# Requesting expert weights into places of the first stage as they come free, and storing the last logits from ScalarE's queue

## The chip, the cores and the metric

The kernel runs on one core of one Trainium2 chip. The metric is the device time of one execution in microseconds (us); the median of several executions is given. TensorE is called PE, VectorE DVE, ScalarE ACT, GpSimd POOL and SyncE SP, as in the profile.

## The reference, cut to what matters

Three parts follow one another, all in float32 (`w_gate`, `w_val` and `w_out` arrive as float64).

```
X = rfft(x, axis=1); y = irfft(X * (filt_r + 1j*filt_i), n=3072)   # x: 8 x 3072 x 256
logits = y @ phi                                                   # 24576 tokens, 32 slots
slot_in = softmax(logits, over tokens).T @ y                       # 32 x 256, 8 experts x 4 slots
slot_out[e] = relu(slot_in[e] @ w1[e]) @ w2[e]                     # w1: 256 x 1024, w2: 1024 x 256 each
z = softmax(logits, over slots) @ slot_out                         # 24576 x 256
out = (silu(z @ w_gate) * (z @ w_val)) @ w_out                     # 256 -> 1536 -> 256
```

The slots need the logits of all tokens, so the experts cannot start until the whole first part is done, and the last part cannot start until the experts are done.

## The kernel before, in words

The program is written in the order in which each engine is to run it (`tc.manual_schedule`): every engine, and each DMA queue with the engine that issues it, takes its own instructions strictly in the order of the text. A DMA that SP issues has SP wait until what the DMA needs is there, and all that SP has still to issue stands behind it.

**First stage, `phase1` (L131).** Sixteen steps (a batch of eight and half of the 256 columns each) of six units, so 96 units, numbered `i` in the loop at L690. A unit does one sixth of a step's spectrum (`s2_unit`, `tr_unit`, `phi_pair`); beside it, units 1 to 4 of a step transform the next step's x (`s1_chunk`, `spread`). x stands in two places `xp[0]` and `xp[1]` (16 KB of each partition), its transforms in `bp[0]` and `bp[1]` (12 KB), with two staging tiles `sgp` (4 KB) between. Three kinds of work are threaded into the units as generators:

- `chain(b)` (L307): for each batch the logits, their maximum, exponentials and slot sums. `pump` (L665) moves it one step on. Its step at L400 to L405 stores the batch's logits to DRAM (`lgd`) in four DMAs on SP's queue.
- `conv` (L558): turns w_gate, w_val and w_out into float32 in DRAM, 12 chunks each, 36 in all. A chunk is four calls: two DVE operations (L584, L585), three ACT operations (L587 to L589), one DVE operation (L591), then two POOL operations, the store on SP's queue and the load of the chunk after next (L593 to L596). One more call at the beginning loads the first two chunks.
- `first_weights` (L599): the softmax over slots of the first batch, 16 calls, after `conv`.

`aside` (L686) makes one call of the generator that is first in the list `side`; a call that finds its generator at the end does no work and takes it off the list. Before the change a unit from 8 on makes one call at L698 and a second at L712 while `conv` is first, or in the last four units; unit 4 makes one. What is left of `side` after the loop is run to its end at L726.

After the loop all places on the right side are given back (L714), the eight w1 tiles are laid over them, four of them are requested (L717), and the tail runs the last units and the chains of batches 6 and 7 (L719 to L728).

**Transition (L731).** SP requests the other four w1, the eight w2 (1 MB each, rows of 1 KB), and the float32 w_gate and w_val (wg, wv, 1.5 MB each), L758 to L768, all by `flat_load` (L128). Then the experts: `stage1` (L777, w1) and `stage2` (L805, w2; experts 0 to 3 come first), after them a 256 x 256 step to w_gate and w_val (L839 to L869), and requests for the first weights `c` (`first`, L882) and w_out. POOL clears `stm` (L770) before `stage1`.

**Last stage, `phase2` (L940).** 576 items of two matmuls of 512 columns and eight that project the result. It begins when the experts are done.

The order of the calls around the change is in these lines:

```
for g in (g7, g7, g7, g6, g7, g6, g7, g7, g6, g7, g6, g6):
    next(g, None)
for _ in g7:
    pass
for g in side:
    for _ in g:
        pass
```

Of the kernel before, what the change touches and what calls it, by code (L numbers as in the profile page):

```python
# [7 lines left out]
F32 = mybir.dt.float32  # L8
# [9 lines left out]
NB, SEQ, D, E = 8, 3072, 256, 32  # L18
NEXP, SPE, FE, FF = 8, 4, 1024, 1536
# [60 lines left out]
def spectral_softmoe_glu_kernel(  # L80
# [17 lines left out]
    nc = tc.nc  # L98
# [20 lines left out]
    c2, c3, p2 = ExitStack(), ExitStack(), ExitStack()  # L119
    w1s = {}  # L120

    def one(shape, name, stack=c2, side="left", dt=F32):

        p = stack.enter_context(tc.tile_pool(name=f"p_{name}", bufs=1, side=side))
        return p.tile(shape, dt, tag=name, name=name)

    def flat_load(dst, src, p):
        nc.sync.dma_start(out=dst, in_=src.rearrange("(t p) f -> p t f", p=p))  # L128


    def phase1():  # L131
        with ExitStack() as c1:

            cr = ExitStack()
            bp = [cr.enter_context(tc.tile_pool(name=f"bp{k}", bufs=1, side="right")) for k in (1, 0)][::-1]
            sgp = cr.enter_context(tc.tile_pool(name="sgp", bufs=2, side="right"))
            xp = []
            cvp = c1.enter_context(tc.tile_pool(name="cvp", bufs=1))
            yp = [c1.enter_context(tc.tile_pool(name=f"yp{k}", bufs=1)) for k in range(3)]
# [23 lines left out]
            def load_x(step, k):  # L163
                b, h = divmod(step, 2)
                if b >= NB:
                    return

                if k == 0:
                    xt[step] = xp[step % 2].tile([128, 2, 16, 128], F32, tag="x", name="x")
                xr = x[b].rearrange("(p h r n) d -> r h p n d", h=2, r=2, n=16)  # L170
                for r in range(2):
                    nc.sync.dma_start(
                        out=xt[step][64 * r:64 * r + 48, k], in_=xr[r, k, :, :, h * 128:(h + 1) * 128]
                    )

            def load_filters(g):

# [129 lines left out]
            def chain(b, last):  # L307
# [43 lines left out]
                for k in range(6):  # L351
                    pe.transpose(
                        out=col(ps, k),
                        in_=lts[:, k // 2, k % 2].rearrange("p ri m -> p (ri m)"),
# [5 lines left out]
                for jj in range(NJ):  # L360
                    g, k = jj % 4, jj // 4
                    pe.matmul(
                        out=col(ps, k)[32 * g:32 * g + 32],
                        lhsT=col(lh, jj, 32),
                        rhs=inv[:, JJ[jj], :],
# [21 lines left out]
                for h in range(2):  # L387
                    for g in range(2):
                        pe.matmul(
                            out=pl[h][64 * g:64 * g + 64].rearrange("p (e n) -> p e n", n=16),  # L390
                            lhsT=i2_sb[64 * h:64 * h + 64, :],
                            rhs=t4[64 * h:64 * h + 64, :, 16 * g:16 * g + 16],
# [6 lines left out]
                yield  # L399
                for h in range(2):  # L400
                    for g in range(2):
                        nc.sync.dma_start(
                            out=lgd[b].rearrange("(n h) g e k -> h g n e k", h=2)[h, g],
                            in_=lg[h][64 * g:64 * g + 48],
                        )  # L405
# [4 lines left out]
                    out=mg, in_=ps[0:32, 0:128].rearrange("p (g n) -> p g n", g=2)[:, :, 0:48], axis=AX.X, op=ALU.max  # L410
# [8 lines left out]
                for h in range(2):  # L419
                    dve.tensor_tensor(  # L420
                        out=dd[:, h],
# [14 lines left out]
                for g in range(2):  # L436
                    for h in range(2):
                        pe.matmul(
                            out=pl[64 * h:64 * h + 64, g],
                            lhsT=s1t_sb[64 * g:64 * g + 48, :],  # L440
                            rhs=dd[64 * g:64 * g + 48, h],
# [6 lines left out]
                for jj in range(NJ):  # L448
                    g, k = jj % 4, jj // 4
                    pe.matmul(  # L450
                        out=col(ps, k)[32 * g:32 * g + 32],
                        lhsT=bd[:, :, JJ[jj]],
                        rhs=fwd[:, JJ[jj], :],
# [24 lines left out]
                for q in range(3):  # L478
                    for ri in range(2):
                        for g in range(4):  # L480
                            pe.matmul(  # L481
                                out=ps[32 * g:32 * g + 32, 0:D],
# [72 lines left out]
            def flat(a):  # L555
                return a.rearrange("(p a) f -> p (a f)", p=128)

            def conv():  # L558


                cw = 256
                chunks = [(i, c) for i in range(3) for c in range(FF * D // 128 // cw)]
                raws = {}

                def load(n):
                    if n >= len(chunks):
                        return
                    i, c = chunks[n]
                    raws[n] = cvp.tile([128, cw, 2], I32, tag="raw", name="raw", bufs=2)
                    nc.sync.dma_start(  # L570
                        out=raws[n].rearrange("p n k -> p (n k)"),
                        in_=flat((w_gate, w_val, w_out)[i])[:, c * cw:(c + 1) * cw].bitcast(I32),
                    )

                load(0)
                load(1)
                yield
                for n, (i, c) in enumerate(chunks):
                    raw = raws.pop(n)
                    hw, lw, lf = raw[:, :, 1], raw[:, :, 0].bitcast(U32), raw[:, :, 0].bitcast(F32)  # L580
                    ex = cvp.tile([128, cw], I32, tag="ex", name="ex", bufs=2)
                    mn = cvp.tile([128, cw], I32, tag="mn", name="mn", bufs=2)
                    mf = mn.bitcast(F32)
                    dve.tensor_scalar(ex, hw, 20, 0x7FF, ALU.logical_shift_right, ALU.bitwise_and)  # L584
                    dve.tensor_scalar(mn, hw, 0xFFFFF, 0x100000, ALU.bitwise_and, ALU.bitwise_or)  # L585
                    yield
                    act.activation(ex, ex, AF.Relu, bias=expo, scale=float(1 << 23))  # L587
                    act.activation(lf, lw, AF.Copy, scale=2.0 ** -32)
                    act.activation(mf, mn, AF.Copy)  # L589
                    yield  # L590
                    dve.scalar_tensor_tensor(ex, hw, -(1 << 31), ex, ALU.bitwise_and, ALU.bitwise_or)  # L591
                    yield
                    pool.tensor_tensor(out=mf, in0=mf, in1=lf, op=ALU.add)  # L593
                    pool.tensor_tensor(out=mf, in0=mf, in1=ex.bitcast(F32), op=ALU.mult)
                    nc.sync.dma_start(out=flat(wd[i])[:, c * cw:(c + 1) * cw], in_=mf)
                    load(n + 2)  # L596
                    yield
# [39 lines left out]
            with tc.tile_pool(name="xp01", bufs=1, side="right") as p01:  # L637
# [11 lines left out]
                for step in range(2):  # L649
                    for c in range(4):  # L650
                        s1_chunk(step, c)
                        spread()
            xp += [cr.enter_context(tc.tile_pool(name=f"xp{k}", bufs=1, side="right")) for k in (1, 0)][::-1]
            dve.memset(ones, 1.0)
            dve.memset(expo, -916.0 * (1 << 23))
            side = [conv(), first_weights()]
            todo = []
            gens, ready = [], []
            units = [(s, u) for s in range(2 * NB) for u in range(6)]
# [30 lines left out]
            for i, (s, u) in enumerate(units):  # L690
                if u in (0, 2):
                    load_x(s + 2, u // 2)
                if i == 6:
                    nc.sync.dma_start(out=inv, in_=c_inv)
                s2_unit(s, u)
                spread()
                tail_ops(i)
                if i >= 8:  # L698
                    aside()
                pump(1)  # L700
                for c in plan[u] if s > 1 else late[u] if s else ():
                    s1_chunk(s + 1, c)
                    if s == 1 and u == 5:
                        spread()
                if u == 5:
                    bt.pop(s)
                if i >= len(units) - 10:
                    pump(1)
                if i == 88:
                    kept(0)  # L710
                    kept(1)
                if i == 4 or i >= 8 and (len(side) > 1 or i >= len(units) - 4):  # L712
                    aside()
            cr.close()  # L714
            for e in reversed(range(NEXP)):
                w1s[e] = one([128, 2, FE], f"w1_{e}", c3, "right")
            for e in range(4):  # L717
                flat_load(w1s[e], w1[e], 128)
            for i in range(len(units), len(units) + 4):  # L719
                tail_ops(i)  # L720
            (_, g6), (_, g7) = gens + ready
# [9 lines left out]
    def transition():  # L731
# [5 lines left out]
        w2s = {}  # L737
# [17 lines left out]
        wg = one([128, 2, FF], "wg")  # L755
        wv = one([128, 2, FF], "wv")

        for e in (4, 5):  # L758
            flat_load(w1s[e], w1[e], 128)
        flat_load(w2s[0], w2[0], 128)  # L760
        for e in (6, 7):
            flat_load(w1s[e], w1[e], 128)
        for e in (6, 7):
            flat_load(w2s[e], w2[e], 128)
        flat_load(wg, wd[0], 128)
        for e in (1, 2, 3, 5, 4):
            flat_load(w2s[e], w2[e], 128)
        flat_load(wv, wd[1], 128)  # L768

# [7 lines left out]
        def stage1(st, ch):  # L777
            ph = bank([128, 512], "h")
            cs = slice(ch * 512, (ch + 1) * 512)
            for d_ in range(2):  # L780
                for i in range(4):
                    e = 4 * st + i
                    pe.matmul(
                        out=ph[32 * i:32 * i + 32, :],
                        lhsT=stm[:, d_, e, :],
                        rhs=w1s[e][:, d_, cs],
                        start=(d_ == 0),
                        stop=(d_ == 1),
                        tile_position=(0, 32 * i),
                    )  # L790
            if ch == 0:
                act.activation(hs[st][:, cs], ph, AF.Relu)
            else:
                dve.tensor_scalar_max(hs[st][:, cs], ph, 0.0)
# [278 lines left out]
```

## Time and profile before

| what | value |
|---|---|
| median of 3 runs | 1540.72 us (1538.58 to 1543.03) |
| the profiled execution, its own time | 1539.64 us |
| its span, first to last instruction | 1537.9 us |
| granted clock of TensorE over the span | 0.991 |
| PE busy | 94% |
| DVE busy | 78% |
| first stage, by the first and last unit's products | 35.7 to about 387 us |
| tail, transition | about 387 to 454 us |
| last stage | 454 us to the end |

Views of the profile used here: the page (shares over the span), the chain that ended last (followed back from the last instruction: what released each step), the timeline of an engine (start, duration, what, and in brackets how long the engine had been idle and who ended it), tables of windows (busy time of each engine in a stretch, the granted clock, the share of time that the 16 DMA engines were busy, and GB/s), and a tile's view (all instructions that read or write it).

### The profile page before, as it was taken

The page shows a single profiled execution, that of the slowest core. Times are in us where ns is not written, and L with a number is a line of the kernel's source. Part 1 is how long each engine was busy: PE and PEld are TensorE (multiplying, and loading weights), DVE is VectorE, ACT ScalarE, POOL GpSimd, SP SyncE. Part 2 cuts the span into 40 slices and gives each one's busy share as a digit, 9 for nine tenths or more (in the row PEclk, how much of TensorE's full clock was granted, in tenths as well). Part 3 has the DMA queues.
Part 4 walks back from the last instruction along what each step waited for, and adds up shares of the span by engine and source line. Part 5 has one row for each costly group of instructions (what it writes and reads, how often), then busy time and mean ns, then how long its engine had stood idle before and what let it go on. Part 6 is the DMA issues. An engine that isn't in the chain of part 4 may idle for free.

```text
span 1537.9 us, 26707 instructions
## 1 busy us (share of the span) xinstructions
PE 1449.9 (94%) x10282; PEld 1133.8 (74%) x10282; DVE 1204.9 (78%) x1976; ACT 955.1 (62%) x1808; POOL 241.3 (16%) x297
## 2 busy tenths in 40 slices
PE   3789998898869999999999999999999999999998
PEld 1455555555438888888888888888888888888887
DVE  3698899898328878887887788788778878877775
ACT  2365565564227666766766677677667667666665
POOL 1566555654010000000000000000000000000000
PEclk9999999999989999999999999999999999999999
DMA  9978678761990120121112013101301310120111
GB/s 193 189 132 147 115 132 142 124 117 56 366 279 25 35 68 19 29 69 27 27 35 71 16 28 69 30 23 35 72 15 29 69 35 18 35 62 14 28 29 28
DMA packets 90482, 116.53 MB, mean 76 GB/s; under 512 B 8657, under 2 KB 69970, under 8 KB 90034
## 3 DMA queue, kind: packets, MB, share of 16 engines
q1 hardware_dynamic: 88882, 111.15, 33.2%
q10 hardware_dynamic: 1216, 3.15, 1.1%
q8 instruction: 81, 1.33, 0.4%
q0 software_dynamic: 256, 0.52, 0.2%
q14 instruction: 47, 0.39, 0.1%
HBM read 68.13 MB, written 34.60 MB: 67 GB/s over the span
## 4 chain that ended last, share of the span: by engine, by line
PE 80%; DVE 11%; DMA 5%; issue 2%; ACT 1%; SPq 1%; POOL 0%; DVEq 0%; ACTq 0%; POOLq 0%
PE o L987 35%; PE o L991 18%; PE V L960 9%; PE G L959 9%; PE X L248 2%; DVE sg L225 2%; DVE P L256 2%; PE s L217 2%; DVE Q L257 2%; DMA fwd<-in_const_fwd_dram 2%; DMA raw<-in_moe_w_gate_dram 1%; PE T L279 1%; PE c L481 1%; DMA w<-in_moe_w_dram 1%; PE L L288 1%
## 5 line engine op out<-in xcount | busy, mean ns | idle before, releaser
L987 PE MATMUL o<-wo,hi 128*128 128x512 f32 x2304 | 831.1, 395 | 0.0
L991 PE MATMUL o<-wo,lo 128*128 128x256 f32 x2304 | 644.6, 280 | 0.2 <-DVE lo L976 0.2
L962 ACT ACTIVATE s<-G 128x512 f32<-128x512 f32 x576 | 344.7, 598 | 317.4 <-PE G L959 314.5
L968 DVE TENSOR_TENSOR h<-V,s 128x512 f32<-128x512 f32 x576 | 395.2, 686 | 168.9 <-ACT s L962 168.1
L987 PEld LDWEIGHTS o<-wo,hi 128*128 128x128 f32 x2304 | 432.0, 187 | 103.4
L991 PEld LDWEIGHTS o<-wo,lo 128*128 128x128 f32 x2304 | 433.6, 188 | 25.9 <-DVE lo L976 0.6
L976 DVE TENSOR_TENSOR lo<-h,hi 128x512 fp32r<-128x512 f32 x576 | 417.1, 724 | 0.1
L975 ACT CAST hi<-h 128x512 fp32r<-128x512 f32 x576 | 354.7, 616 | 12.5 <-DVE h L968 9.2
L960 PE MATMUL V<-c,v 128*128 128x512 f32 x576 | 227.4, 395 | 2.1 <-DVE h L968 1.8
L959 PE MATMUL G<-c,g 128*128 128x512 f32 x576 | 227.9, 396 | 0.0
L248 PEld LDWEIGHTS X<-b,fwd 128*64 128x64 f32 x1536 | 83.2, 138 | 67.9 <-issue 50.2
L959 PEld LDWEIGHTS G<-c,g 128*128 128x128 f32 x576 | 108.1, 188 | 25.6 <-issue 0.8
L234 ACT COPY b<-sg 128x768 f32<-128x768 f32 x64 | 58.7, 918 | 102.6 <-DVE sg L225 102.3
L225 DVE STREAM_TRANSPOSE sg<-s 128x1024 f32<-128x1024 f32 x64 | 78.9, 1236 | 47.9 <-PE s L217 47.9
L248 PE MATMUL X<-b,fwd 128*64 128x128 f32 x1536 | 106.3, 281 | 10.5 <-ACT b L234 5.0
L960 PEld LDWEIGHTS V<-c,v 128*128 128x128 f32 x576 | 108.6, 189 | 4.2 <-DVE h L968 2.9
L906 POOL TENSOR_TENSOR lg<-lg,mx 96x1024 f32<-96x1024 f32 x7 | 16.9, 2418 | 581.1 <-DVE mx L904 581.1
L217 PE MATMUL s<-x,csm 48*64 48x512 f32 x512 | 73.3, 628 | 34.2 <-DMA x<-in_x_dram 21.1
L1001 DVE TENSOR_TENSOR ot<-o,tmp 128x256 f32<-128x256 f32 x192 | 70.0, 423 | 39.5 <-ACT tmp L1000 39.5
L269 POOL TENSOR_TENSOR y<-P 128x256 f32<-128x256 f32 x96 | 70.2, 731 | 144.5 <-DVE P L256 144.5
L271 POOL TENSOR_TENSOR y<-Q 128x256 f32<-128x256 f32 x95 | 77.4, 815 | 0.9 <-DVE Q L259 0.8
L281 ACT COPY yt<-T 128x512 f32<-128x512 f32 x96 | 55.9, 582 | 30.4 <-PE T L279 29.9
(195 smaller groups left out, 1017.6 us busy)
## 6 DMA issues: line engine op xcount, KB each, us to landing
out_dram<-ot SPq DMA_DIRECT2D x192, 128.0 KB, 2.2
x<-in_x_dram SPq DMA_DIRECT2D x56, 384.0 KB, 8.2
w<-in_moe_w_dram SPq DMA_DIRECT2D x16, 1024.0 KB, 12.4
c<-ch SPq DMA_DIRECT2D x42, 128.0 KB, 2.4
c<-cl SPq DMA_DIRECT2D x42, 128.0 KB, 2.4
raw<-in_moe_w_gate_dram SPq DMA_DIRECT2D x12, 256.0 KB, 4.5
lgd<-lg SPq DMA_DIRECT2D x32, 96.0 KB, 6.9
raw<-in_moe_w_val_dram SPq DMA_DIRECT2D x12, 256.0 KB, 3.7
```

Of the source, the lines that this page charges most:

```text
L217: pe.matmul(out=ps[64 * k:64 * k + 64, 16 * r:16 * r + 16, :], lhsT=s1t_sb[64 * r:64 * r + 48, :], rhs=xt[step][64 * r:64 * r + 48, k, :, ...
L225: dve.transpose(out=sg.rearrange("p j d k -> p d j k"), in_=ps.rearrange("p n d -> p d n"))
L248: pe.matmul(out=ps[par * 64:(par + 1) * 64, i, ri, :], lhsT=fwd[:, j, ri * 64:(ri + 1) * 64], rhs=bb[:, j, :],)
L271: eng.tensor_tensor(out=y[:, :, 1, :], in0=Q[:, :, 0, :], in1=Q[:, :, 1, :], op=ALU.add)
L959: pe.matmul(out=pg, lhsT=g4[c][:, fs], rhs=c4[b][:, q, G, :])
L960: pe.matmul(out=pv, lhsT=v4[c][:, fs], rhs=c4[b][:, q, G, :])
L962: act.activation(s, pg, AF.Silu)
L968: dve.tensor_tensor(out=h, in0=pv, in1=s, op=ALU.mult)
L975: act.copy(hi, h)
L976: dve.tensor_tensor(out=lo, in0=h, in1=hi, op=ALU.subtract)
L987: pe.matmul(out=a, lhsT=hi[:, ts], rhs=wo[f].rearrange("p k d -> p (k d)"), start=(f == 0), stop=(f == NF - 1), skip_group_check=True,)
L991: pe.matmul(out=a[:, D:2 * D], lhsT=lo[:, ts], rhs=wo[f][:, 0, :], start=False, stop=(f == NF - 1), skip_group_check=True,)
```

## The change

- The pools of x, its transforms and the staging tiles are kept open until the experts' first half is done, and w1 is put into tiles of these pools in halves of 0.5 MB (`w1s[e, d_]`). Each is requested when the place's last reader stands in the text: four halves in `xp[0]` in unit 83, four in `xp[1]` in unit 89, two in `sgp` and three in `bp[0]` in unit 90, and three in `bp[1]` after the loop.
- The logits of batches 6 and 7 are stored from ACT's queue.
- `conv` is split: w_gate and w_val first, then `first_weights`, then w_out. The second call is made in unit 4 and in every unit from 8 on that isn't the last of its step (`u` 5).
- In the transition SP requests no w1, and w2 in another order: 6, 7, wg, 5, 0, 4, 1, 2, 3, wv.

```diff
-            cr = ExitStack()
-            bp = [cr.enter_context(tc.tile_pool(name=f"bp{k}", bufs=1, side="right")) for k in (1, 0)][::-1]
-            sgp = cr.enter_context(tc.tile_pool(name="sgp", bufs=2, side="right"))
+            bp = [c3.enter_context(tc.tile_pool(name=f"bp{k}", bufs=1, side="right")) for k in (1, 0)][::-1]
+            sgp = c3.enter_context(tc.tile_pool(name="sgp", bufs=2, side="right"))
...
+            def expert_places(p, shape, tag, parts):
+
+                t = p.tile(shape, F32, tag=tag, name="w1")
+                for i, (e, d_) in enumerate(parts):
+                    w1s[e, d_] = t[:, i * FE:(i + 1) * FE] if len(shape) == 2 else t[:, i, :]
+                    nc.sync.dma_start(out=w1s[e, d_], in_=w1[e, 128 * d_:128 * d_ + 128, :])
...
-                        nc.sync.dma_start(
+                        (nc.scalar if b >= NB - 2 else nc.sync).dma_start(
                             out=lgd[b].rearrange("(n h) g e k -> h g n e k", h=2)[h, g],
                             in_=lg[h][64 * g:64 * g + 48],
                         )
...
-            def conv():
+            def conv(kinds):
...
-                chunks = [(i, c) for i in range(3) for c in range(FF * D // 128 // cw)]
+                chunks = [(i, c) for i in kinds for c in range(FF * D // 128 // cw)]
...
-            side = [conv(), first_weights()]
+            side = [conv((0, 1)), first_weights(), conv((2,))]
...
+                if i == len(units) - 13:
+                    expert_places(xp[0], [128, 4, FE], "x", [(0, 0), (0, 1), (1, 0), (1, 1)])
+                if i == len(units) - 7:
+                    expert_places(xp[1], [128, 4, FE], "x", [(2, 0), (2, 1), (3, 0), (3, 1)])
+                if i == len(units) - 6:
+                    for d_ in range(2):
+                        expert_places(sgp, [128, FE], "sg", [(4, d_)])
+                    expert_places(bp[0], [128, 3, FE], "b", [(5, 0), (5, 1), (6, 0)])
                 if i >= len(units) - 10:
                     pump(1)
...
-                if i == 4 or i >= 8 and (len(side) > 1 or i >= len(units) - 4):
+                if i == 4 or i >= 8 and u < 5:
                     aside()
-            cr.close()
-            for e in reversed(range(NEXP)):
-                w1s[e] = one([128, 2, FE], f"w1_{e}", c3, "right")
-            for e in range(4):
-                flat_load(w1s[e], w1[e], 128)
+            expert_places(bp[1], [128, 3, FE], "b", [(6, 1), (7, 0), (7, 1)])
...
-        for e in (4, 5):
-            flat_load(w1s[e], w1[e], 128)
-        flat_load(w2s[0], w2[0], 128)
-        for e in (6, 7):
-            flat_load(w1s[e], w1[e], 128)
         for e in (6, 7):
             flat_load(w2s[e], w2[e], 128)
         flat_load(wg, wd[0], 128)
-        for e in (1, 2, 3, 5, 4):
+        for e in (5, 0, 4, 1, 2, 3):
             flat_load(w2s[e], w2[e], 128)
         flat_load(wv, wd[1], 128)
...
-                        rhs=w1s[e][:, d_, cs],
+                        rhs=w1s[e, d_][:, cs],
```

## Rows read from the trace of the kernel before

**Rows 1.** The page: the span, and the chain that ended last, by engine.

```profile
span 1537.9 us, 26707 instructions
...
PE 80%; DVE 11%; DMA 5%; issue 2%; ACT 1%; SPq 1%; POOL 0%; DVEq 0%; ACTq 0%; POOLq 0%
```

**Rows 2.** The chain that ended last, 412 to 450 us: start us, us, what.

```profile
418.90 17.78 DMA w<-in_moe_w_dram
...
436.72 3.37 PE o L808 x26
...
440.68 1.86 PE o L808 x32
...
446.79 0.38 ACT so L832
```

**Rows 3.** Timeline of SP's queue: start us, us, line, DMA, count.

```profile
365.47 0.87 SPq L513 DMA_DIRECT2D slots<-sld  x2
366.43 0.38 SPq L607 DMA_DIRECT2D lgf<-lgd  x1
...
384.16 2.62 SPq L128 DMA_DIRECT2D w<-in_moe_w_dram  x4
395.10 1.74 SPq L402 DMA_DIRECT2D lgd<-lg  x4
396.88 13.23 SPq L128 DMA_DIRECT2D w<-in_moe_w_dram  x7
```

**Rows 4.** Timelines of DVE, POOL, PE and ACT, 384 to 424 us.

```profile
410.37 0.42 DVE L535 TENSOR_TENSOR rb<-csm,beta 128x256 f32<-128x256 f32 x1
413.50 0.22 DVE L775 COPY stm<-a 128x64 f32<-128x64 f32 x1 [2.70 <-PE a L773]
...
385.13 0.52 POOL L770 MEMSET stm<- 128x512 f32 x1
...
422.09 0.62 PE L808 MATMUL o<-w,ht 128*32 128x256 f32 x2
...
398.89 1.23 ACT L426 ACTIVATE dd<-dd 128x512 f32<-128x512 f32 x2 [2.56 <-DVE dd L420]
```

**Rows 5.** Views of raw and mn: count, ns min/median/max, first and last start; landing us.

```profile
L584 DVE TENSOR_SCALAR ex<-raw x36: 275/498/799, 55.9 to 324.1; 128x256 int32<-128x256 int32 x36
L585 DVE TENSOR_SCALAR mn<-raw x36: 279/818/833, 56.1 to 324.3; 128x256 int32<-128x256 int32 x36
...
L591 DVE SCALAR_TENSOR_TENSOR ex<-raw,ex x36: 556/570/579, 57.5 to 327.7; 128x256 int32<-128x256 int32 x36
L593 POOL TENSOR_TENSOR mn<-mn,raw x36: 722/737/920, 58.6 to 328.8; 128x256 f32<-128x256 f32 x36
...
DMA to landing us min/median/max: 2.7/4.2/11.4
...
L594 POOL TENSOR_TENSOR mn<-mn,ex x36: 725/732/792, 59.4 to 329.6; 128x256 f32<-128x256 f32 x36
```

**Rows 6.** Windows: us, busy of PE, PEld, DVE, ACT, POOL, clock, DMA share, GB/s.

```profile
387.00:396.00 9.00, 7.17 (x126) 4.71 (x122) 3.62 (x8) 3.77 (x10) 0.00 (x0) 1.00 1.02 409
...
423.00:432.00 9.00, 1.06 (x2) 0.18 (x2) 0.00 (x0) 0.00 (x0) 0.00 (x0) 0.67 1.07 290
432.00:438.00 6.00, 2.34 (x14) 0.77 (x18) 0.00 (x0) 0.00 (x0) 0.00 (x0) 0.50 1.10 350
```

**Rows 7.** Views of tiles w (landing) and c (requests of ACT's queue).

```profile
DMA to landing us min/median/max: 5.4/12.4/18.9
...
L886 ACTq DMA_DIRECT2D c<-cd x2: 340/396/453, 421.6 to 422.0; - x2
```

**Rows 8.** Windows of the first stage: twelve units, then units 68 to 70 and 80 to 82.

```profile
276.61:322.64 46.03, 41.74 (x537) 24.95 (x533) 42.09 (x71) 26.70 (x57) 27.01 (x37) 1.00 0.76 133
283.94:297.92 13.98, 11.30 (x139) 6.23 (x139) 13.98 (x22) 7.72 (x15) 6.54 (x9) 1.00 0.90 156
329.97:341.06 11.09, 10.63 (x134) 5.95 (x134) 11.09 (x18) 5.68 (x9) 4.82 (x7) 1.00 0.73 141
```

More of the change, by code (lines that the diff above doesn't have):

```diff
@@ L652, in phase1 @@
                         spread()
-            xp += [cr.enter_context(tc.tile_pool(name=f"xp{k}", bufs=1, side="right")) for k in (1, 0)][::-1]
+            xp += [c3.enter_context(tc.tile_pool(name=f"xp{k}", bufs=1, side="right")) for k in (1, 0)][::-1]
             dve.memset(ones, 1.0)
             dve.memset(expo, -916.0 * (1 << 23))
-            side = [conv(), first_weights()]
+            side = [conv((0, 1)), first_weights(), conv((2,))]
             todo = []
```

## The prediction, made before the changed kernel ran

> **What bounds the kernel now.** I read the page first: the chain that ended last is PE for 80% of the span of 1537.9 us, DVE for 11%, DMA for 5% [rows 1]. The change touches only the first 454 us, so next I read the chain around the transition. There the last wait is on weights: from 418.90 it waits 17.78 us for a w2, PE goes on with the experts' second half (L808) at 436.72, and the experts' output is copied at 446.79 [rows 2]. PE had reached this second half at 422.09 [rows 4], so 14.6 us are lost to late w2 (that of expert 3 lands last of the four that the first products need). SP's timeline shows what stood ahead of them: four w1 at 384.16, then the four stores of the last logits, which SP could issue only at 395.10, then the other weights from 396.88 [rows 3]. The windows show that from 387 on the DMA engines are full: share 1.02 at 409 GB/s for w1, 1.10 at 350 GB/s for w2 [rows 6]. So bytes bound the transition, and weights that arrive earlier ought to end it earlier.
>
> In the first stage twelve units take 46.03 us, with DVE busy 42.09 and PE 41.74 [rows 8]: neither alone bounds it, and which of them is last changes from unit to unit.
>
> **The calls decide SP's order.** The diff also changes how often the side generators are called, and that has to be counted. After the change there is one call in unit 4; of the units 8 to 95, 88 make the first call, and 88 less 15 (units 11, 17, ... 95) the second: 1 + 88 + 73 = 162. The generators need 98 calls for w_gate and w_val (1 + 24 x 4, and one that finds the end), 17 for the first weights, and 49 for w_out (1 + 12 x 4): 164. So two calls are left over after the loop: the second DVE operation of w_out's last chunk (L591), and its POOL operations with the store on SP (L593 to L595). They run at L726, after the whole tail. The same counting for the kernel before (one call in unit 4, two a unit from 8 to 79, one from 80) puts the second load of the first weights into unit 89; SP's timeline has it at 366.43, right behind the loads of unit 88 (slots) at 365.47 [rows 3]. I trust the counting.
>
> SP takes its work in the order of the text. The store of that last chunk stands ahead of every w2, wg, wv and of c and w_out. It waits for POOL, POOL for DVE, and DVE's operation stands behind the tail's last one, which starts at 410.37 and takes 0.42 [rows 4]. So the change takes away a wait of SP at 395 (for the last logits) and puts one at 413 in its place, in front of all w2.
>
> **The transition, step by step.**
> - SP is free: 410.79 + 0.57 + 0.74 + 0.73 [rows 5], and hand-overs and the store's issue of about 0.5: 413.3.
> - The DMA engines are then empty, as all w1 have been requested by 385 and at 409 GB/s 1.57 MB take 4 us. From a request into empty queues to a landing: a w1 took at least 5.4 us [rows 7]; less 1.05 MB at 409 GB/s, 2.6 us, this leaves 2.8.
> - In the new order w2 of expert 3 is the last but wv. Before it go 7 others and wg: 8 x 1.05 MB at 350 GB/s are 24.0 us, wg 1.57 MB at 409 (long rows, as w1) 3.8 us.
> - c, requested by ACT at 421.6 [rows 7], shares the engines: in 423 to 432 they moved 2.61 MB at 290 GB/s [rows 6], of which 0.79 were c; the other 1.82 MB would have taken 5.2 us at 350, so c cost 3.8.
> - Landing: 413.3 + 2.8 + 24.0 + 3.8 + 3.8 = 447.7. PE went on at 436.72 before, so **+11.0 us**. What follows is unchanged: in both kernels all other weights of the second half are there then, and PE begins after a wait at the lower of its two clock levels (0.50 granted at 432 to 438, 1.2 GHz [rows 6]).
>
> Bounds: all w2 and wg at w1's 409 GB/s with c behind them, 413.3 + 2.8 + 24.4 = 440.5, +3.8; everything with c at 290, 10.75 MB in 37.1 us, 453.2, +16.5. I take 350, the row of w2 alone. By the Trainium skill ("DMA: Bandwidth & Descriptors", Specifications) a core gets about 358 GB/s from HBM; the w1 row at 409 GB/s is above that, so it is no ceiling here; by it the 10.75 MB would take 30.0 us instead of 31.6.
>
> Where something costs nothing, its cover is this. Sixteen halves of w1 instead of eight whole: 0.66 us each to issue (2.62 for 4 [rows 3]) on SP, which is waited for by the side chunks alone; they are fetched two ahead, so a chunk can come late only in the last units (below). The four stores on ACT: 0.40 us each by its nearest row [rows 7], 1.6 us together, in 2.56 us in which ACT was idle ahead of the exponential at 398.89 [rows 4]; were that cover gone, 1.6. Those of batch 6 lie in the units, where ACT is busy for 26.70 of 46.03 [rows 8]. POOL's clearing of stm, 0.52 us done at 385 before, now stands behind the last chunk and ends at about 413.4, when DVE needed it at 413.50 [rows 4]: 0 to 0.5.
>
> **The first stage.** A chunk costs DVE 0.50 + 0.82 + 0.57 = 1.89 us [rows 5], 0.47 a call.
> - Up to unit 79 there are 12 calls fewer (units 11 to 77): 5.7 us of DVE. DVE and PE are about equally long [rows 8], so I take half, -2.8 (bounds 0 and -5.7).
> - From unit 80 on, 29 calls of w_out now stand where 16 light ones were. Units 80 to 82 took 11.09 us without a chunk, the same places of the step 13.98 with [rows 8]: +2.9. The later units had idle time from the first weights' own chain, which goes. Bounds 0 and 13.7 (all 29 on the path).
> - In unit 70 the first two chunks of w_out are requested and used in one unit: landing takes 4.2 us [rows 5], about half a unit lies between, and DVE waits with everything behind it; in unit 94 the last chunk stands behind 2.6 MB of w1. +1.5 (bounds 0 and 9.5, the longest landing less half a unit).
> - Sum **+1.6**, in practice -3 to +5.
>
> **Sum.** 11.0 + 1.6 = 12.6. The profiled execution took 1539.64 us, so 1552.2; the median shown is 1.08 above it: **1553.3 us**.
>
> **The rivals.**
> - *SP isn't held (faster).* If the last chunk were stored inside the loop, SP could ask for w2 right behind the last w1 at 385. 384.2 + 2.8 + 3.8 (rest of w1) + 24.0 + 3.8 + 3.8 = 422.4, about when PE gets there. Three quarters of the second half took 440.68 to 446.79 at full clock [rows 2], so all of it 8.1, done at 430.5: -16.3, with +1.6 gives 1526. It decides by two calls: were 164 made, or the store behind the weights. For it speaks that this is what the requests in the units are laid out for; against it the count, which the load at 366.43 bears out. 0.06.
> - *The held requests run faster (no change).* With nothing else under way w2 moves at w1's rate, c comes behind, and DVE's relief counts in full: +3.8 - 5.7 + 2.9 = +1.0, 1541.7. For it: DMA was crowded in every row that I have of w2. Against it: at 432 to 438 w2 was alone and moved at 350. 0.08.
> - *It is slower still.* w2 and c disturb each other throughout (290): +16.5 + 1.6, 1558.8. Against it: c is only 0.79 MB. 0.10.
>
> **How the numbers follow.** The forecast has 0.76. 0.3%, 4.6 us, is about what a measurement of this kernel can tell from no change. Faster: the first rival, 0.06. Within: the second, and a little of the forecast's low end, 0.09. Slower: 0.85. The range goes from the forecast with the first stage at -3 and a w2 rate near 380 (about 1545) to the third rival, 1559; outside are the two first rivals and some 0.05 at the ends. I put the low end at 1544.
>
> **What would show it.** Right: SP's store to wod (L595) at about 413 and the first w2 right behind it; DMA share near 0 from about 391 to 414; PE's wait for w at L808 some 10 us longer, ending at 446 to 449; no wait of stage 1 for w1; last unit within 3 us of before. Wrong: w2 requested from 385 on (the count failed), or w2 at 350 GB/s no longer (the rate failed), or the last unit over 5 us away (the first stage failed).

## The result, and the profile after

The changed kernel took **1560.82 us** (median of 4 runs, 1559.07 to 1565.41), the kernel before 1541.88 in the same comparison: a ratio of 1.0131, 95% interval 1.0102 to 1.0159. It is slower, as forecast, but 7.5 us above the forecast and above the range, which ended at 1559. The profiled execution took 1559.07 us. Its page gives the span, and the shares of the chain that ended last:

```profile
span 1557.3 us, 26681 instructions
...
PE 81%; DVE 9%; DMA 5%; ACT 2%; SPq 2%; issue 1%; POOL 0%; DVEq 0%; ACTq 0%; POOLq 0%
```

The span grew by 19.4 us, yet these shares are those of [rows 1] within two points. What a stage lost can't be read from them; it is read at points that both traces have. (Lines are numbered 5 or 6 higher than before from L180 on: L595 is now L601, L808 is L813.)

**The transition first.** SP's queue: start us, us, line, DMA, count.

```profile
384.01 0.38 SPq L576 DMA_DIRECT2D raw<-in_moe_w_out_dram  x1
388.26 0.33 SPq L601 DMA_DIRECT2D wod<-mn  x1
388.68 1.34 SPq L180 DMA_DIRECT2D w<-in_moe_w_dram  x3
420.25 0.33 SPq L601 DMA_DIRECT2D wod<-mn  x1
420.68 1.09 SPq L128 DMA_DIRECT2D w<-in_moe_w_dram  x2
421.86 1.51 SPq L128 DMA_DIRECT2D wg<-wgd  x1
423.54 23.47 SPq L128 DMA_DIRECT2D w<-in_moe_w_dram  x6
```

Between the last w1 (388.68) and the first w2 (420.68) there is one store of w_out. Before, SP could issue the stores of the last logits, its next requests behind the first four w1, at 395.10, and the rest of the weights from 396.88 [rows 3]. What the store waited for stands in the timelines of DVE and POOL (in brackets how long the engine was idle, and who ended it):

```profile
418.60 0.42 DVE L541 TENSOR_TENSOR rb<-csm,beta 128x256 f32<-128x256 f32 x1
418.94 0.42 DVE L597 SCALAR_TENSOR_TENSOR ex<-raw,ex 128x256 int32<-128x256 int32 x1
421.72 0.23 DVE L780 COPY stm<-a 128x64 f32<-128x64 f32 x1 [2.37 <-PE a L778]
...
392.43 0.92 POOL L599 TENSOR_TENSOR mn<-mn,raw 128x256 f32<-128x256 f32 x1
419.50 0.73 POOL L600 TENSOR_TENSOR mn<-mn,ex 128x256 f32<-128x256 f32 x1 [26.15 <-DVE ex L597]
420.17 0.52 POOL L775 MEMSET stm<- 128x512 f32 x1
```

This is the left-over work of the count: DVE does the chunk's last operation behind the tail's last one (`rb`), POOL has waited 26.15 us for it, and SP stores 0.02 us after POOL ends. In the meantime the DMA engines stood still. Windows of the changed kernel: us, busy of PE, PEld, DVE, ACT, POOL, clock, DMA share, GB/s.

```profile
387.00:393.00 6.00, 1.21 (x14) 0.58 (x12) 2.40 (x6) 1.60 (x4) 2.42 (x4) 0.68 0.97 339
396.00:402.00 6.00, 4.99 (x115) 3.81 (x114) 2.36 (x6) 1.85 (x5) 0.00 (x0) 1.00 0.00 0
408.00:420.00 12.00, 10.46 (x163) 5.34 (x156) 5.18 (x18) 2.44 (x7) 0.50 (x1) 0.93 0.01 1
429.00:432.00 3.00, 1.39 (x12) 0.42 (x4) 1.29 (x2) 0.00 (x0) 0.00 (x0) 1.00 1.00 410
432.00:441.00 9.00, 0.00 (x0) 0.00 (x0) 0.00 (x0) 0.00 (x0) 0.00 (x0) 0.59 1.08 265
441.00:453.00 12.00, 2.10 (x5) 0.37 (x5) 0.00 (x0) 0.00 (x0) 0.00 (x0) 0.50 1.09 348
```

A share of 0.00 and 0.01 while all eight w2 are still to be requested: it isn't bytes that hold the experts there but requests. The Trainium skill ("DMA: Bandwidth & Descriptors", Anatomy of one DMA — SWDGE (gpsimd) path) has it that DMA engines never wait for a semaphore, the engine that issues does, before it hands the transfer over. It says so of GpSimd's path; on SP's queue here the empty windows agree. PE's timeline, behind all this (two more such waits, of 5.03 and 1.95 us, lie between the two lines):

```profile
443.92 1.03 PE L813 MATMUL o<-w,ht 128*32 128x256 f32 x2 [13.54 <-issue]
...
455.97 3.62 PE L813 MATMUL o<-w,ht 128*32 128x256 f32 x26 [1.92 <-DMA w<-in_moe_w_dram]
```

PE goes on at 455.97 where it was 436.72 [rows 2], 19.25 later. Of this 8.22 were there when DVE copied `stm` (421.72 against 413.50 [rows 4]), so from there to the second half the transition lost **11.0 us**, the term of the forecast. The other **8.2 us** were lost in the first stage and the tail, where the forecast had 1.6.

**Then the first stage.** A unit begins when DVE starts its multiplication P (L256 before, L262 after); DVE's timeline has 96 of them. The time between some of these starts, in us (the last three columns are experiments, described below; "units 8 to 56" is from the start of unit 8 to that of 56):

| stretch | before | after | calls alone | calls as before | halves later |
|---|---|---|---|---|---|
| start of unit 8 | 52.10 | 52.37 | 54.32 | 53.32 | 51.92 |
| units 8 to 56 | 185.80 | 184.63 | 184.62 | 185.25 | 183.60 |
| units 56 to 80 | 92.07 | 94.79 | 94.72 | 92.06 | 94.83 |
| units 80 to 94 | 51.12 | 52.78 | 51.50 | 51.41 | 52.38 |
| unit 94 | 2.61 | 6.41 | 3.14 | 2.61 | 3.14 |

The start of unit 8 differs from run to run by up to 2 us and tells nothing of the change. After against before: -1.17, +2.72, +1.66 and +3.80. Of the +1.66 the kernel with the calls alone has 0.38; the other 1.28 lie in units 87 to 88, and no run takes apart which of the changed kernel's further requests makes them. Unit 94 is in the chain that ended last:

```profile
384.01 6.53 DMA raw<-in_moe_w_out_dram
390.57 0.31 DVE ex L590
...
391.37 0.42 ACT raw L594
391.79 0.30 ACT mn L595
392.09 0.48 ACT yt L287
392.71 1.08 PE T L285 x4
```

The last load of `raw` took 6.53 us, behind w1 requested from 379.64 (the window from 387 still has the engines 0.97 full); DVE stood for it for 4.39 us, then ACT turned the chunk (0.72 us) before its next copy `yt`. PE, idle for 4.79 us by then, went on at the lower of its two clock levels: 0.50 granted (1.2 GHz) from 390.50 to 394.00, where before it had 1.00 from 381 to 393. The four products T took 1.08 us instead of 0.74.

```profile
390.50:394.00 3.50, 1.29 (x6) 0.90 (x8) 2.48 (x6) 1.72 (x5) 1.60 (x2) 0.50 0.98 366
```

### The profile page after: what moved, and what is told of

Its sections match the earlier page's. It is cut to its first block, busy times and chain, and to the rows that moved or that the text cites. A ratio compares the mean times of both kernels' runs of the same rounds, so it can differ in the third digit from the quotient of the medians.

```text
span 1557.3 us, 26681 instructions
## 1 busy us (share of the span) xinstructions
PE 1454.1 (93%) x10282; PEld 1135.5 (73%) x10282; DVE 1197.4 (77%) x1976; ACT 954.7 (61%) x1808; POOL 240.2 (15%) x297
## 4 chain that ended last, share of the span: by engine, by line
PE 81%; DVE 9%; DMA 5%; ACT 2%; SPq 2%; issue 1%; POOL 0%; DVEq 0%; ACTq 0%; POOLq 0%
PE o L992 34%; PE o L996 17%; PE V L965 9%; PE G L964 9%; PE X L254 3%; DVE sg L231 2%; PE s L223 2%; PE T L285 2%; DMA fwd<-in_const_fwd_dram 2%; PE c L487 1%; DVE P L262 1%; SPq L128 1%; DVE Q L263 1%; PE L L294 1%; DMA raw<-in_moe_w_gate_dram 1%
```

## The experiments

Each kernel was run beside the kernel before; the ratio is to that.

| kernel | median us | ratio to before, 95% interval |
|---|---|---|
| the changed kernel | 1560.82 | 1.0131, 1.0102 to 1.0159 |
| e1 store before the tail | 1538.74 | 0.9973, 0.9963 to 0.9982 |
| e2 halves after raw | 1557.36 | 1.0092, 1.0075 to 1.0109 |
| e3 both | 1535.77 | 0.9949, 0.9934 to 0.9965 |
| e4 calls as before | 1530.88 | 0.9925, 0.9905 to 0.9945 |
| e5 order of w2 | 1525.31 | 0.9887, 0.9872 to 0.9901 |
| e6 logits on SP | 1538.05 | 0.9970, 0.9957 to 0.9983 |
| e7 calls alone | 1559.74 | 1.0114, 1.0095 to 1.0133 |
| e8 held, old order | 1555.99 | 1.0086, 1.0071 to 1.0101 |
| e9 call in every unit | 1532.27 | 0.9938, 0.9922 to 0.9955 |
| e10 that and the order | 1529.45 | 0.9907, 0.9892 to 0.9922 |

Differences between kernels are given below as those of the ratios, times 1542 us.

**e1: the left-over calls ahead of the tail.** The changed kernel with the lines that run `side` to its end moved.

```diff
             expert_places(bp[1], [128, 3, FE], "b", [(6, 1), (7, 0), (7, 1)])
+            for g in side:
+                for _ in g:
+                    pass
             for i in range(len(units), len(units) + 4):
                 tail_ops(i)
...
-            for g in side:
-                for _ in g:
-                    pass
```

> The changed kernel with the two leftover calls of the last w_out chunk made right behind the last three halves of w1, ahead of the tail instead of behind it. Theory (the store of that chunk holds SP, and so all w2, until the tail is over): SP is free at about 392 to 394, the wait of PE for w at L813 goes from some 26 us to under 2, the experts' output is copied at 438 to 442 instead of 466.9, and the time falls by 25 to 28 us to 1533 to 1536 us. Rival A (the weights are late because the transfers themselves are slow or in a worse order): under 5 us of change, 1556 to 1561. Rival B (the early halves or the four stores on ACT's queue cost the time): no change.

Measured: 24.4 us less than the changed kernel, a little under the range, and a copy of the experts' output at 445.06 instead of 438 to 442. SP's queue has the store at its new place, and w2 behind it:

```profile
387.80 1.36 SPq L180 DMA_DIRECT2D w<-in_moe_w_dram  x3
393.50 0.33 SPq L601 DMA_DIRECT2D wod<-mn  x1
393.92 1.29 SPq L128 DMA_DIRECT2D w<-in_moe_w_dram  x2
399.56 0.37 SPq L128 DMA_DIRECT2D wg<-wgd  x1
413.22 12.76 SPq L128 DMA_DIRECT2D w<-in_moe_w_dram  x6
```

Two calls at the wrong place cost 24 us: the hold is the cause of the transition's loss, and of more, since without it the change gains. PE's last wait for w2 is 2.35 us. What is new, and what the expectation lacked, is the gap from 399.56 to 413.22: SP is held a second time (e4 shows by what).

**e2: the halves of unit 90 requested in unit 92**, behind the last load of `raw`.

```diff
-                if i == len(units) - 6:
+                if i == len(units) - 4:
```

> The changed kernel with the five halves of w1 of unit 90 requested in unit 92, behind the load of w_out's last chunk; the store stays behind the tail. Theory (the last chunk's load queues behind 2.6 MB of w1, and DVE, with PE behind it, waits for it from 386.2 to 390.6): that wait goes, the last unit starts 4 to 5 us earlier, and the time falls by 4 to 5 us to 1554.5 to 1557. Rival (the load is late since SP issues it late, behind the store of the chunk before; then the halves don't matter): the wait stays over 3 us and the time within 1.5 us of the changed kernel's.

Measured: 6.0 us less by the ratios, a little more than expected. In the trace unit 94 takes 3.14 us instead of 6.41, so 3.3 us of it are shown in their place; the intervals leave room for the rest. The 2.72 us of units 56 to 80 stay (94.83).

**e3: both of these.**

> Both edits of the two runs before. If the two costs stand one behind the other (the load's wait in the last units, the store's hold in the tail), the gains add up: 29 to 33 us under the changed kernel, 1528 to 1532 us, 10 to 14 us under the kernel before. If the halves requested two units later then come too late for the first experts, PE waits for w at L788 and the sum is some us less.

Measured: 28 us under the changed kernel and 7.9 under before, short of the ranges (29 to 33, 10 to 14); the two gains, 24.4 and 6.0, nearly add.

**e4: the calls of the kernel before**, all else changed.

```diff
-            side = [conv((0, 1)), first_weights(), conv((2,))]
+            side = [conv((0, 1, 2)), first_weights()]
...
-                if i == 4 or i >= 8 and u < 5:
+                if i == 4 or i >= 8 and (len(side) > 1 or i >= len(units) - 4):
```

> The changed kernel with the order of the side generators and the number of their calls as before the change (nothing is left over, and no chunk is loaded beside the halves of w1). Theory: the first stage ends within 2 us of where it did before the change, SP asks for w2 at 386, the second half of the experts does not wait for over 2 us, and the time is 14 to 17 us under the kernel before: 1525 to 1528 us. Rival (the early requests of w1 slow down the last units or the tail by themselves): the last unit over 3 us later than before the change, and 1530 us or more.

Measured: 11.6 us under before, some 3 short. The first stage is as before to 0.6 us in each stretch. What is short lies behind it, in the tail and in SP's second wait; SP's longest in the table of waits, 380 to 430 us (us in total, times, longest), and PE's wait for w2 in its timeline:

```profile
SPq L128 <- PE cl L487: 11.6, 1, 11.6
```

```profile
429.60 2.58 PE L813 MATMUL o<-w,ht 128*32 128x256 f32 x26 [2.33 <-DMA w<-in_moe_w_dram]
```

The w2 of expert 5 goes into a place that the chain of batch 6 reads until PE's L487, and the changed order puts it ahead of five others, that of expert 0 among them, whose place is free. A window of this kernel has the DMA engines idle again while that lasts:

```profile
402.00:408.00 6.00, 5.74 (x52) 1.63 (x48) 2.47 (x5) 1.25 (x3) 0.00 (x0) 0.60 0.06 21
```

The same line shows PE busy at a granted clock of 0.60. Ahead of it PE had been busy for 0.28 us of 398 to 400, at a granted clock of 0.99. This kernel's tail is 3.1 us longer from the start of unit 95 to the product `a`, from which `stm` is copied, than that of before (32.20 against 29.06); why its clock was lower, no run here tells.

**e5: e4 with w2 in an order that asks for free places first**: 6, 7, 0, wg, 1, 2, 3, 5, 4, wv.

```diff
-        for e in (6, 7):
+        for e in (6, 7, 0):
...
-        for e in (5, 0, 4, 1, 2, 3):
+        for e in (1, 2, 3, 5, 4):
```

> The kernel with the calls as before (e4), and w2 requested in the order 6, 7, 0, wg, 1, 2, 3, 5, 4. In e4 SP stood from 393.3 to 407.8 us at the w2 of expert 5, whose place is read by the chain of batch 6 until then, and that of expert 0, whose place is free, stood behind it; expert 3's landed last, at 429.6, and PE waited 2.3 us and then ran at the lower clock level (13.6 us from 426.19 to the copy at about 439.8, against 8.1 at full clock). Theory: with expert 0 ahead of that wait and expert 3 two transfers earlier PE does not wait at L813 at all, and the second half takes 8 to 10 us: 4 to 6 us under e4, a ratio of 0.988 to 0.990 to the kernel before. Rival (the wait of SP for the place decides whatever the order): within 1.5 us of e4.

Measured: the range is hit, 1525.31 us, the fastest of all and 1.1% under before. SP and PE:

```profile
383.26 1.34 SPq L180 DMA_DIRECT2D w<-in_moe_w_dram  x3
384.71 5.62 SPq L128 DMA_DIRECT2D w<-in_moe_w_dram  x3
390.74 3.17 SPq L128 DMA_DIRECT2D wg<-wgd  x1
403.54 9.06 SPq L128 DMA_DIRECT2D w<-in_moe_w_dram  x5
```

```profile
422.21 1.93 PE L813 MATMUL o<-w,ht 128*32 128x256 f32 x32
...
424.66 1.93 PE L813 MATMUL o<-w,ht 128*32 128x256 f32 x32
```

No wait in brackets is left at L813, and 32 products take 1.93 us where 26 took 3.62 in the changed kernel. SP still waits until 403.54 for a place, again for L487 and now with expert 1, but it does so with enough bytes ahead of it: the engines are 1.01 busy until then. In the traces 2.1 us of the gain over e4 lie in the tail (30.14 us against 32.20), where the clocks differ; e10 against e9, whose tails both take 29.17, shows the order's gain without that.

```profile
391.00:403.50 12.50, 10.20 (x127) 5.15 (x125) 6.64 (x15) 4.16 (x10) 0.00 (x0) 0.86 1.01 354
```

**e6: e4 with the last logits stored by SP again.**

```diff
-                        (nc.scalar if b >= NB - 2 else nc.sync).dma_start(
+                        nc.sync.dma_start(
```

> The kernel with the calls as before (e4), with the last logits stored by SP again. Then SP issues them at 397 to 399 us in the tail, and w2 of experts 6 and 7 and wg (3.7 MB, 10 us) behind them instead of from 386.6 on. If the wait for the place at 407.8 us is what then holds the rest of w2, the three are nearly through by then and the change to ACT's queue is worth 0 to 2 us. If every us in which w2 is asked for later counts, it is worth 10 us.

Measured: 6.9 us slower than e4, between the two figures. SP asks for its first w2 at 398.54, behind the four stores:

```profile
396.70 1.74 SPq L408 DMA_DIRECT2D lgd<-lg  x4
398.54 1.13 SPq L128 DMA_DIRECT2D w<-in_moe_w_dram  x2
...
405.20 16.21 SPq L128 DMA_DIRECT2D w<-in_moe_w_dram  x6
```

The wait for the place ends at 405.20 here, but now bytes come last: w2 of expert 3 is needed at 424 and PE gets it at 433.98, about what the forecast's own sum gives from 398.54 (+ 2.8 + 24.0 + 3.8 + 3.8 = 432.9). So ScalarE's queue is worth some 7 us where nothing else holds SP. In the changed kernel, where the store came later than the logits anyway, it should be worth nothing; that is argued, no run has it alone.

**e7: the kernel before with the new calls alone** (`conv` takes its kinds, as in the change).

```diff
-            side = [conv(), first_weights()]
+            side = [conv((0, 1)), first_weights(), conv((2,))]
...
-                if i == 4 or i >= 8 and (len(side) > 1 or i >= len(units) - 4):
+                if i == 4 or i >= 8 and u < 5:
```

> The kernel before with the new split and number of calls alone: w1 as whole tiles behind the loop, logits on SP, w2 in the old order; two calls are left over and run behind the tail. Theory (the hold by the left-over store costs the time, and the early w1 then brings nothing): the last chunk's load finds empty queues, so the first stage ends 3 to 5 us later than before the change and not 8; SP then asks at about 416 us for four w1 and w2, and expert 3's w2 lands at 453 to 456; 1556 to 1561 us, within 4 us of the changed kernel. Rival (the early requests are what costs): 1541 to 1547 us.

Measured: hit, 1559.74. Nothing of the weights' requests is changed here, and yet the loss is there; in SP's queue the store is in front of the w1 and w2 that were still to be requested:

```profile
415.66 0.34 SPq L595 DMA_DIRECT2D wod<-mn  x1
416.05 12.18 SPq L128 DMA_DIRECT2D w<-in_moe_w_dram  x7
```

The early w1 and ScalarE's queue, taken together, can't be told from nothing beside the hold (1.0131 against 1.0114, intervals overlap).

**e8: the changed kernel with w2 in the order of before**: 0, 6, 7, wg, 1, 2, 3, 5, 4, wv; the hold stays.

```diff
-        for e in (6, 7):
+        for e in (0, 6, 7):
...
-        for e in (5, 0, 4, 1, 2, 3):
+        for e in (1, 2, 3, 5, 4):
```

> The changed kernel with w2 in the order of before (0, 6, 7, wg, 1, 2, 3, 5, 4). SP is held as in the changed kernel, to about 420.6 us. Theory (bytes behind the hold decide): expert 3's w2 has two transfers of 3.0 us less ahead of it, PE goes on at L813 some 6 us earlier (449 to 451), the last two land while it works on the first four, and the time falls by 4 to 7 us to 1554 to 1557 us. Rival (the second half as a whole waits for the last byte): within 1.5 us of the changed kernel.

Measured: 6.9 us less by the ratios, at the upper end (1.9 by the two profiled executions, the slowest of this kernel and the fastest of the changed one). In its trace SP stores at 422.79 and PE goes on at 453.87, 31.1 us later, where the changed kernel takes 35.7 from 420.25: expert 3 is then sixth of the w2 instead of last.

**e9 and e10: the changed kernel with a second call in every unit from 8 on**, e10 with e5's order too.

```diff
-                if i == 4 or i >= 8 and u < 5:
+                if i == 4 or i >= 8:
```

> The changed kernel, but with a second call in every unit from 8 on, those that are the last of a step included; the split of the side work stays. Count: 1 + 2 x 82 = 165 calls by unit 89, so all 164 are made inside the loop and SP isn't held. Both theories: last w1 and first two w2 requested right behind each other at about 386, then the wait for the place of the w2 of expert 5, as with the calls of before: some 27 to 31 us less than the changed kernel, 10 to 12 under before. They differ in units 57 to 80, where the changed kernel and the kernel with its calls alone lost 2.7 us against before. Theory A, the first weights ahead of w_out cost it (their 16 calls take DVE longer than a chunk's): they stand in units 57 to 65 here, the 2.7 us stay, units 56 to 80 take 94.7 us (before 92.07) and the time is 1533. Theory B, the skipped calls cost it by moving the chunks' operations against the units: units 56 to 80 take 92.1, and the time is 1531 or less.

> The same with w2 requested in the order 6, 7, 0, wg, 1, 2, 3, 5, 4, so that no w2 waits for the place that batch 6's chain holds ahead of others with free places. Expected as with the calls of before: 5 to 6 us less than without the order, so 1525 to 1528, and no wait of PE for w2.

Measured: e9 is 1532.27, between the two; the times don't part the theories, the trace does: units 56 to 80 take 94.62 us (A: 94.7, B: 92.1). The split costs these 2.6 us also when no call is skipped; with the order of before (e4) they are gone. e10 is 4.8 us under e9 by the ratios (expected 5 to 6), its median a little above the expected 1525 to 1528, and PE doesn't wait for w2. This is the smallest mend of the changed kernel; e5 is better still, by 3.1 us by ratios whose intervals overlap, and by as much at the start of unit 95 in the traces (382.74 against 385.88).

## Why the prediction was right and wrong

**Right: what holds SP.** The count (162 of 164 calls), the store behind the tail, DMA engines empty until it, PE's wait at L813: all as written, some 7 to 8 us later, and e1, e7 and e9 show that it is the cause, by taking it away in two ways and by making it alone.

**Right, by two errors that cancel: +11.0 us.** From `rb`'s start to SP being free I took 2.93 us (410.37 to 413.3); it took 1.98 (418.60 to 420.58), because POOL had done its first operation (L599) long before, at 392.43, and DVE's took 0.42 instead of 0.57. From there to the landing I took 34.4; it took 35.4. The rates held: w2 at 348 GB/s (350 taken), the stretch of wg at 410 (409 taken); c's share is the part that can hold the 1.0, with 265 GB/s in 432 to 441 where I had 290 from [rows 6]. That the two errors cancel is luck. The Trainium skill ("DMA: Bandwidth & Descriptors", Specifications) gives a core some 358 GB/s from HBM; the 410 of wg is above it, and w2, with rows of 1 KB, stayed under it where it moved alone.

**Right: the zeros.** The four stores on ACT ended well before the exponential, whose wait was still for DVE; POOL had cleared `stm` by 420.69, and DVE copied into it at 421.72. This row of ACT's timeline answers to [rows 4]:

```profile
407.11 1.23 ACT L432 ACTIVATE dd<-dd 128x512 f32<-128x512 f32 x2 [2.57 <-DVE dd L426]
```

**Wrong: the first stage, +1.6 forecast, +8.2 measured up to `stm`.** The last unit began 7.3 us later than before (390.98 against 383.70), past the 5 us that the prediction gave as the sign of this failure. Two of its steps failed.
- *"Up to unit 79 there are 12 calls fewer ... I take half, -2.8."* Up to unit 56 the relief was there, -1.17 us (the kernel with the calls alone: -1.18). But between units 56 and 80 the changed kernel lost 2.72 us, so that the sum to unit 80 was +1.55 instead of -2.8. I counted calls and not which work moved into these units: with the split the first weights' 16 calls come there, in front of w_out. I called them light. The rows of DVE's timeline in the changed kernel say otherwise; those of one of the two groups:

```profile
263.36 1.00 DVE L617 TENSOR_REDUCE mx<-lgf 96x16 f32<-96x512 f32 x1
...
265.45 0.65 DVE L262 TENSOR_TENSOR P<-X,ft 128x512 f32<-128x512 f32 x1
...
266.62 1.02 DVE L623 TENSOR_REDUCE sm<-lgf 96x16 f32<-96x512 f32 x1
267.68 0.17 DVE L624 TENSOR_SCALAR sm<-sm 96x16 f32<-96x16 f32 x1
267.88 0.25 DVE L625 RECIPROCAL sm<-sm 96x16 f32<-96x16 f32 x1
...
269.59 1.07 DVE L629 STREAM_TRANSPOSE ctf<-lgf 96x512 f32<-96x512 f32 x1 [0.35 <-POOL lgf L626]
270.59 0.64 DVE L262 TENSOR_TENSOR P<-X,ft 128x512 f32<-128x512 f32 x1
...
272.92 0.64 DVE L634 TENSOR_TENSOR ctf<-ctf,chf 96x512 fp32r<-96x512 f32 x1
```

Without the two P, which begin units 63 and 64, these make 4.15 us, so 8.3 for 16 calls or 0.52 a call: not light, but only 0.8 us above 16 calls of a chunk at 0.47. The rest is where they fall. Unit 63 takes 5.14 us here, with 2.51 us of them in it, and took 2.83 before, when DVE was busy throughout with one 0.57 us operation of a chunk (window of the kernel before):

```profile
266.31:269.14 2.83, 2.83 (x33) 1.68 (x31) 2.83 (x6) 2.17 (x4) 2.11 (x3) 1.00 1.25 131
```

By the start of unit 70, when the first weights are done, 2.0 of the 2.7 us are lost. e4 and e9 show that the split makes these 2.6 us; that it is long operations falling together in units where DVE is full is read from the rows, and no run moved single calls.
- *"In unit 94 the last chunk stands behind 2.6 MB of w1. +1.5."* The place was right and the size wrong: unit 94 alone lost 3.80 us, of which e2 gave back 3.3. The bound in the text, 9.5, held it, but I took one value near the low end for two units. (In unit 70, the other one, DVE did not wait for a landing: 4.37 us against 4.79 before.) It could have been worked out: five halves are 2.62 MB, at 409 GB/s [rows 6] 6.4 us, and with the 2.8 from a request to its landing they last until 388.8 when requested at 379.64; `raw` landed at 390.54.

Units 80 to 94 lost 1.66 where I had 2.9 for them, which was too much (0.38 in the kernel with the calls alone). Beyond these, the tail from unit 95 to `a` took 0.95 longer, and unit 8 began 0.27 later. Of the 0.95, 0.80 lie between the last products T (start 385.35 before, 392.71 now) and the next step of the chain (L352 at 387.36, L358 at 395.52), the stretch at a granted clock of 0.50.

**Not foreseen, small.** PE goes on from the lower of its two clock levels (0.50 granted in 441 to 453, 1.2 GHz), as before, but has more of the second half at it: from 455.97 to the copy of the experts' output at 466.87 it takes 10.90 us at a mean granted clock of 0.78, before 10.07 [rows 2] at 0.85, +0.8. What follows gave back 0.7. In sum: 8.2 + 11.0 + 0.8 - 0.7 is 19.4 with rounding, the growth of the span.

**The first rival had its price right for another reason.** It put the kernel with SP not held at 1526. e9, which makes just that true, is at 1532.27, and e4, with the calls of before, at 1530.88, as the w2 of expert 5 waits for its place; I had priced w2 back to back and not looked up when their places come free. With e5, e4 in another order, that wait is covered and the time is 1525.31, without the +1.6 that the rival had included.

## What to carry to other kernels

Where work is threaded into a loop in calls, count the calls against the turns: what is left over runs at the end, and a store among it holds every load behind it on the same queue. Order the loads of a queue by when their places come free as well as by when they are needed. A small load that compute needs soon goes ahead of big prefetches on its queue; and work that moves in time is placed unit by unit with its own rows on the engine that is full there, not priced by its number of calls or by their mean.

## What the runs showed of the hardware that was not expected

- The same gap in PE's work can be followed by either clock level. In e4 PE idled for 1.49 and 0.78 us before 400.35 (granted clock 0.99 in 398 to 400, PE busy for 0.28 of 2.00 us) and then had 0.50 from 402 to 406, busy for all of it. In the kernel with the calls alone it idled for 1.48 and 0.78 us before 402.31 and had 1.00 from 396 to 416. No run here separates what made the difference.
- c beside w2 costs more than its bytes at w2's rate: with both under way the engines were 1.08 busy and moved 265 GB/s, w2 alone 348 at 1.09.
